# Sliding-window attention and a gated convolution feed-forward: token halves in the lead-in, two-bank score tiles, and convolution blocks that change engine

## The chip, the cores and the metric

The kernel runs on one core of one Trainium2 chip. Its engines work in parallel, each on its own queue and in the order of that queue: TensorE (PE) multiplies matrices, VectorE (DVE), ScalarE (ACT) and GpSimd (POOL) work element by element, and SyncE (SP) issues the transfers between the chip's memory and the cores' working memory. They wait for each other through semaphores. PE writes its results to PSUM, eight banks of 512 fp32 numbers for each of 128 partitions; ACT and DVE read them there. The metric is the device time of one execution in microseconds; the median of several executions counts.

## The reference, cut to what matters

```python
# q, k, v: (8, 8, 576, 64) fp32 = batch, heads, tokens, head size
scores = (q @ k.T) / sqrt(64)                  # each token sees the tokens within 32 of it
scores = where(abs(i - j) <= 32, scores, -1e9)
attn = exp(scores - max); attn = attn / sum(attn)
x = (attn @ v), heads side by side             # (8, 576, 512)

h = maximum(x @ w_in, 0)                       # w_in: 512 x 1024
conv = w[0]*h[t-1] + w[1]*h[t] + w[2]*h[t+1]   # per channel, 3 taps, zero outside
out = (h * sigmoid(conv)) @ w_out              # w_out: 1024 x 512, out fp32
```

## The kernel before, in words

**Attention of one batch.** The tokens go in tiles of 64 queries against 128 keys, because the window is 32 to each side. q and k come in through SP as fp32, are cast to bf16 by POOL (`cast_qk`, lines 286 to 287), and turned by PE with an identity (`tr_mm`) so that the head size lies on the partitions; ACT and DVE copy the turned tiles out of PSUM (`tr_copy`), ACT five of nine rows and DVE four. v is cast by POOL (`cast_v`), and a copy of it, moved by 64 tokens, is made for the odd tiles (`shift_v`, tile `vo`). A "pair" is two heads, in the two halves of the partitions. `sc_mm` computes the scores of eight of the nine tiles of a pair into two PSUM banks, one for each head, `scl_mm` those of the ninth tile of two pairs; ACT takes the exponential, one instruction for each bank (`sc_exp`, `scl_exp`); DVE multiplies with a 0/1 mask (`sc_mask`). `av_mm` (batches 2 to 7) multiplies with v, which has a column of ones beside it, so that the sum of the exponentials comes out as a 65th column; DVE takes its reciprocal (`sum_rec`) and multiplies (`av_norm`), one of each for each head. The result `xn` is turned into `xT`: for batches 2 to 7 by a transposing transfer on SP's queue (`xt_dma`), for batches 0 and 1 by PE and ACT (`xt_mm`, `xt_copy`). In these two the multiplication with v goes by blocks of 128 tokens over all heads (`avc_mm`, `avc_norm`).

**Feed-forward.** Two batches make three chunks of 384 tokens, so there are twelve chunks. For each of the eight blocks `m` of 128 channels, `ph_mm` gives x @ w_in (four matmuls), ACT writes the relu to `hT`, the convolution follows, ACT takes a tanh, and DVE makes the gated product `gT` (`gate`). Then `py_mm` multiplies with w_out, three times eight matmuls, ACT copies the result (`y_copy`) and SP stores it. Chunks 0 and 1 go in two halves of 192 tokens.

**Three ways of the convolution** (`conv_by`, lines 824 to 827). On PE, three matmuls of 384 columns with diagonal matrices (`pc_mm`; the 24 diagonals are made by ACT, `make_diag`). On DVE, ACT makes the first tap and DVE adds two more (`conv_acc`). On POOL, five instructions in working memory (`conv_pool`). Chunks 0 and 1 have all blocks on PE; in the others the lists of lines 820 to 822 decide.

**What sets the order.** No order is written out. Every step is given to a planner (`Planner`, lines 27 to 136) with its engine, an estimated duration, a due time (`want`) and what it depends on. The planner lays the steps out over the engines with these estimates: among the steps that could start first it takes the one that is due first. It also hands out the PSUM banks (`takes`, `gives`) and puts filler matmuls on PE (`fill`) where PE would be idle in the first 30 us. The instructions are then issued in that order on each engine. So a change of estimates or due times (`want_of_b`, `chunk_at`, `S2`, `POOL_LAG`) changes the order everywhere. Loads of q, k, v and the weights stand in one list (`loads`, lines 646 to 656) and go to SP's queue in its order: all of batch 0, w_in, all of batch 1, w_out, and then batch by batch. There is one staging tile for each of q and k halves and for v blocks, so a load waits for the cast of the batch before.

The instructions all carry line 214, that of the helper which issues them; they are told apart by their tiles.

Of the kernel before, what the change touches and what calls it, by code (L numbers as in the profile page):

```python
# [26 lines left out]
class Planner:  # L27
# [16 lines left out]
    def run(self, fill, until):  # L44
# [17 lines left out]

        def slots_at(op):
            at = 0.0
            for name, n in op.takes:
                pool = self.free[name]
                if len(pool) < n:
                    return None
                at = max(at, pool[n - 1][0])
            return at  # L70

        done = 0
        while done < len(ops):
# [30 lines left out]
            for name, n in op.takes:  # L104
                got = self.held[key, name] = [self.free[name].pop(0)[1] for _ in range(n)]
                self.after.setdefault(key, []).extend(self.given.get((name, x)) for x in got)
# [33 lines left out]
def kernel(  # L140
# [27 lines left out]
    ROWS = 2  # L168
# [13 lines left out]
    qT_pp = [pp.tile([128, 2, S], BF16, name=f"qT{i}") for i in range(2)]  # L182
    kT_pp = [pp.tile([128, 2, S + 2 * PAD], BF16, name=f"kT{i}") for i in range(2)]
# [5 lines left out]
    rec_pp = [pp.tile([128, 8], FP32, name=f"rec{i}") for i in range(6)]  # L189
# [12 lines left out]
    warm = pp.tile([128, 512], BF16, name="warm")  # L202
    pf = [psum.tile([128, 512], FP32, name=f"pf{i}") for i in range(8)]
# [29 lines left out]
    scalar.activation(warm[:, 256:512], warm[:, 0:256], AF.Exp, bias=0.0, scale=0.0)  # L233
# [13 lines left out]
    for t_ in kT_pp:  # L247
        vector.memset(t_[:, :, 0:PAD], 0.0)
        vector.memset(t_[:, :, PAD + S:], 0.0)
# [20 lines left out]
    QK, V96, V128, WQ = 1.55, 1.0, 1.2, 1.45  # L270
# [52 lines left out]
    def head(pr, e):  # L323
        return 4 * (pr // 2) + pr % 2 + 2 * e

    def rows_of(part):
        return range(CUT) if part == 0 else range(CUT, RP)

    def tr_mm(b, y, i, part, ps):
        nat = qkb_pp[b % 2][y][i]  # L330
        for n, j in enumerate(rows_of(part)):
            tensor.transpose(
                pf[ps[0]][:, :].bitcast(BF16)[:, 128 * n:128 * n + 128],
                nat[:, j, :, :].rearrange("p e d -> p (e d)"), ident,
            )

    def tr_copy(b, y, i, part, engine, ps):
        js = rows_of(part)
        t_ = (qT_pp, kT_pp)[y][(2 * b + i) % 2]
        to = (t_ if y == 0 else t_[:, :, PAD:PAD + S]).rearrange(  # L340
            "p y (x j) -> p y x j", j=RP)[:, :, :, js[0]:js[-1] + 1]
        from_ = pf[ps[0]][:, :].bitcast(BF16)[:, 0:128 * len(js)].rearrange(
            "p (j y x) -> p y x j", j=len(js), y=2)
# [5 lines left out]
    def score(gi, z, e, t, to):  # L349
        qT, kT = qT_pp[gi % 2], kT_pp[gi % 2]  # L350
        tensor.matmul(
            to,
            kT[64 * e:64 * e + 64, z, 64 * t:64 * t + 128],
            qT[64 * e:64 * e + 64, z, 64 * t:64 * t + 64],
# [13 lines left out]
    def sc_exp(g, e, ps):  # L368
        scalar.activation(
            attn_pp[g // 2 % 2][:, g % 2, e, 0:512], pf[ps[e]], AF.Exp, bias=0.0, scale=scale  # L370
        )

    def scl_exp(gi, e, ps):
        scalar.activation(
            attn_pp[gi % 2][:, :, e, 512:576],
            pf[ps[e]][:, 0:128].rearrange("p (z x) -> p z x", z=2), AF.Exp, bias=0.0, scale=scale,
# [7 lines left out]
    def av_mm(g, ps):  # L384
# [3 lines left out]
        for e in range(2):  # L388
            for c in range(NBLK):
                for j in range(2):  # L390
# [4 lines left out]
                        (ve if t % 2 == 0 else vo)[:, t // 2, head(pr, e), :],  # L395
# [7 lines left out]
    def av_norm(g, e, ps, r):  # L403
        b, pr = g // NP, g % NP
        po = pf[ps[e]][:, 0:65 * NBLK].rearrange("p (c x) -> p c x", x=65)
        rec = rec_pp[r][:, 0:NBLK]
        vector.tensor_tensor(
            out=xn_pp[b % 2][:, :, head(pr, e), :], in0=po[:, :, 0:64],
            in1=rec[:, :, None].broadcast_to([128, NBLK, 64]), op=ALU.mult,
        )  # L410

    def avc_mm(b, c, e, ps):
        ve, vo = ve_pp[b % 2], vo_pp[b % 2]
        for pr in range(NP):
            attn = attn_pp[pr // 2][:, pr % 2]
            for j in range(2):
                t = min(2 * c + j, NT - 1)
                tensor.matmul(
                    pf[ps[0]][64 * j:64 * j + 64, 65 * pr:65 * pr + 65],
                    attn[:, e, 64 * t:64 * t + 64],  # L420
                    (ve if t % 2 == 0 else vo)[:, t // 2, head(pr, e), :],
                    start=True, stop=True,
                )

    def avc_norm(b, c, e, ps, r):
        po = pf[ps[0]][:, 0:65 * NP].rearrange("p (a g x) -> p a g x", a=2, g=2)
        rec = rec_pp[r][:, 0:NP]
        to = xn_pp[b % 2][:, c, :, :].rearrange("p (a e g) d -> p e a g d", a=2, e=2)[:, e]
        vector.tensor_tensor(
            out=to, in0=po[:, :, :, 0:64],  # L430
            in1=rec.rearrange("p (a g) -> p a g", a=2)[:, :, :, None].broadcast_to([128, 2, 2, 64]),
# [49 lines left out]
    def relu(c, m, part, ps):  # L481
# [14 lines left out]
        scalar.activation(to, from_, AF.Relu, bias=0.0, scale=0.5)  # L496
# [83 lines left out]
    NSH = 8  # L580
    VP = 2
# [6 lines left out]
    MO, ME = 7.0, 9.0  # L588
# [3 lines left out]
    S2 = 52.0  # L592
# [10 lines left out]
    DIAG_T = 14.0  # L603
# [28 lines left out]
    for m in range(MB):  # L632
        for kk in range(3):
            engine = "ACT"
# [6 lines left out]
    loads = []  # L641

    def add_load(key, cost, fn, deps=()):
        add(key, "SP", -1.0, 0.5, fn, deps, dma=cost)

    for b in range(B):
        for i in range(NPH):
            for y in range(2):
                loads.append((("load", b, y, i), QK, lambda b=b, y=y, i=i: load_qk(b, y, i),
                              [("cast", b - 1, y, i)]))  # L650
        for c in range(NBLK):
            loads.append((("loadv", b, c), V96 if c in (0, NBLK - 1) else V128,
                          lambda b=b, c=c: load_v(b, c), [("castv", b - 1, c)]))
        if b < 2:
            for x in range(4):
                loads.append((("load w", b, x), WQ, None, [("setup sp",)]))

    return_to = {}

    def want_of_b(b):  # L660

        if b == 0:
            return 4.0, 14.0
        if b == 1:
            return 18.0, 34.0
# [5 lines left out]
    for n, (key, cost, fn, deps) in enumerate(loads):  # L671
# [5 lines left out]
        else:  # L677
            at = 0.01 * n if b < 2 else want_of_b(b)[0] - 22.0 + (n - 8) % 13 * LD
            add(key, "SP", at, 0.5, fn, deps + [("issue", prev), ("setup sp",)]
# [18 lines left out]
    for b in range(B):  # L698
# [3 lines left out]
        avs = lambda bb: ([("avc", bb, c, e) for c in range(NBLK) for e in range(2)] if bb < 2  # L702
                          else [("av", bb * NP + p) for p in range(NP)])
        for i in range(NPH):
            for y in range(2):
                add(("cast", b, y, i), "POOL", t0 + 2 * i * d - 6.0 + y, 1.16,
                    lambda b=b, y=y, i=i: cast_qk(b, y, i),
                    [("load", b, y, i)] + [("tr", b - 2, y, i, part) for part in range(2)] + ([("setup pool",), ("setup dve",)]))
        for c in range(NBLK):
            add(("castv", b, c), "POOL", t0 - 2.0 + 1.5 * c, 0.6, lambda b=b, c=c: cast_v(b, c),  # L710
                [("loadv", b, c), ("vo", b - 2, 0), ("vo", b - 2, 1)]
                + [("voc", b - 2, x, h) for x in range(NBLK - 1) for h in range(2)] + avs(b - 2))
        if b < NSH:
            for c in range(NBLK - 1):
                for h in range(2):
                    engine = ("DVE", "ACT")[(c + h) % 2] if b == 0 else "POOL" if b >= VP else "DVE"
                    add(("voc", b, c, h), engine, t0 + 0.5 * c + (2.0 if engine == "POOL" else 9.0),
# [9 lines left out]
        for i in range(NPH):  # L727
            gi = 2 * b + i
            before = avs(b - 1) if 0 < b < 3 else [("av", 2 * gi - 4), ("av", 2 * gi - 3)]
            used = [("sc", 2 * gi - 4), ("sc", 2 * gi - 3), ("scl", gi - 2)]  # L730
            for y in range(2):
                tt = t0 + 2 * i * d + 0.35 * d * y
                for part in range(2):
                    n = 128 * len(rows_of(part))
# [15 lines left out]
            for e in range(2):  # L750
                add(("expl", gi, e), "ACT", ts + 0.02 + 0.01 * e, act(128),
                    lambda gi=gi, e=e: scl_exp(gi, e, ps_of(("scl", gi))),
                    [lk] + before, gives=[("p", lk, e)])
            for z in range(2):
# [5 lines left out]
                for e in range(2):  # L760
                    add(("exp", g, e), "ACT", ts + 0.01 * e, act(512),
                        lambda g=g, e=e: sc_exp(g, e, ps_of(("sc", g))),
                        [sk] + before, gives=[("p", sk, e)])
# [3 lines left out]
                    [("exp", g, e) for e in range(2)] + [("expl", gi, e) for e in range(2)]  # L767
                    + [("setup pool",)], shared=True)
                if not cmajor:
# [7 lines left out]
                    for e in range(2):  # L777
                        rk = ("rec", g, e)
                        add(rk, "DVE", ta + 0.01, 0.11,
                            lambda r, ak=ak, e=e: sum_rec(NBLK, ps_of(ak)[e], r[0]), [ak],  # L780
                            takes=[("rec", 1)])
                        add(("norm", g, e), "DVE", ta + 0.02, dve(320),
                            lambda g=g, e=e, ak=ak, rk=rk: av_norm(g, e, ps_of(ak), held[rk, "rec"][0]),
                            [rk] + [("xt", b - 2, c) for c in range(NBLK)],
                            gives=[("p", ak, e), ("rec", rk, 0)])
        for c in range(NBLK):
            xdeps = [("ph", (b // 2 - 2) * 3 + z, m, part) for z in range(3) for m in range(MB)
                     for part in (None, 0, 1)]
            if cmajor:
                tx = t1 + 0.9 * c  # L790
                for e in range(2):
                    ak = ("avc", b, c, e)
# [175 lines left out]
```

## Time and profile before

| | us |
|---|---|
| median of 3 runs | 230.41 (229.62 to 232.28) |
| the profiled execution | 230.19 |
| its span, first to last instruction | 228.3 |

| engine | busy us | share of the span | instructions |
|---|---|---|---|
| PE | 216.6 | 95% | 2633 |
| ACT | 194.2 | 85% | 460 |
| POOL | 178.8 | 78% | 202 |
| DVE | 176.2 | 77% | 407 |

The profile is of one execution. A row names the engine, the operation, the tile that is written and those that are read, and the shape. In the rows of groups stand the count, after the bar the busy time and the mean duration of one, and after the second bar the idle time of the engine just before them with what ended it. Matmuls are pipelined and the ends that the profile shows are modelled, so a busy PE can be one that waits shortly between matmuls. "Granted clock" (PEclk) is the share of TensorE's full clock that the chip allowed.

### The profile page before, as it was taken

The numbers are of one execution on the slowest core, as the hardware profiler recorded it, in microseconds if no ns is written. First come the engines' busy times: TensorE is split into PE (matmuls) and PEld (weight loads), VectorE is DVE, ScalarE is ACT, GpSimd is POOL, SyncE is SP. The second block draws the span as 40 slices with busy tenths as digits, with TensorE's granted clock in tenths as the row PEclk, the third lists the DMA queues.
The fourth block names the chain that finished last, engine by engine and source line by source line (L and its number), as shares of the span: only waits on it lengthen the run. The fifth ranks groups of instructions, "written<-read, shape, count | busy, mean of one in ns | idle before, by whom it ended". The sixth has DMA issues, their size and how long they took to land.

```text
span 228.3 us, 6942 instructions
## 1 busy us (share of the span) xinstructions
PE 216.6 (95%) x2633; PEld 140.1 (61%) x2656; DVE 176.2 (77%) x407; ACT 194.2 (85%) x460; POOL 178.8 (78%) x202
## 2 busy tenths in 40 slices
PE   7887997999999999999999999999999999999994
PEld 6786986868665555656555565555556555555542
DVE  4389279769779897959889799859889898877620
ACT  4979799967989878999899898899899978989841
POOL 5574766878989939998989999899789679899400
PEclk9999799999999999999999999999999999999999
DMA  6999999989971579979989487569936403421213
GB/s 227 298 229 377 330 224 354 383 177 296 304 185 46 95 258 342 200 173 328 318 232 289 103 221 194 95 215 318 240 88 103 141 15 95 137 93 46 92 49 138
DMA packets 69590, 45.95 MB, mean 201 GB/s; under 512 B 53533, under 2 KB 55861, under 8 KB 69557
## 3 DMA queue, kind: packets, MB, share of 16 engines
q1 hardware_dynamic: 69520, 45.49, 70.2%
q8 instruction: 21, 0.34, 0.7%
q14 instruction: 13, 0.10, 0.1%
q10 hardware_dynamic: 36, 0.01, 0.0%
HBM read 32.52 MB, written 9.44 MB: 184 GB/s over the span
## 4 chain that ended last, share of the span: by engine, by line
PE 72%; POOL 7%; DVE 7%; ACT 4%; DMA 4%; issue 3%; SPq 1%; DVEq 0%; POOLq 0%; ACTq 0%
PE pf L214 72%; DMA kst<-in_k_dram 4%; POOL vo L214 3%; DVE gT L214 2%; POOL ca L214 1%; ACT hT L214 1%; ACT pf L214 1%; POOL ve L214 1%; DVE pf L214 1%; DVE attn L214 1%; DVE vo L214 1%; POOL cb L214 1%; ACT attn L214 1%; POOL kb L214 1%; SPq L214 1%
## 5 line engine op out<-in xcount | busy, mean ns | idle before, releaser
L214 PE MATMUL pf<-xT,w_in_sb 128*128 128x385 bf16 (+3 forms) x448 | 77.7, 309 | 1.6 <-DVE gT L214 0.8
L214 DVE SCALAR_TENSOR_TENSOR gT<-pf,hT 128x384 bf16<-128x384 f32 (+1 forms) x112 | 53.5, 495 | 19.1 <-ACT pf L214 18.3
L214 PE MATMUL pf<-w_out_sb,gT 128*128 128x512 bf16 (+1 forms) x273 | 66.1, 373 | 1.2
L214 ACT ACTIVATE hT<-pf 128x385 bf16<-128x385 f32 (+3 forms) x112 | 49.8, 465 | 5.9 <-PE pf L214 5.0
L214 PEld LDWEIGHTS <-w_in_sb 128*128 128x128 bf16 x448 | 40.5, 99 | 20.3 <-issue 1.9
L214 ACT ACTIVATE pf<-pf 128x384 f32<-128x384 f32 (+1 forms) x100 | 43.5, 448 | 4.3 <-PE pf L214 2.4
L214 PEld LDWEIGHTS <-gT 128*128 128x128 bf16 x296 | 28.4, 98 | 28.8
L214 ACT ACTIVATE attn<-pf 128x512 bf16<-128x512 f32 (+1 forms) x96 | 41.4, 509 | 0.9 <-PE pf L214 0.8
L214 DVE SCALAR_TENSOR_TENSOR pf<-hT,conv_w_sb,pf 128x384 f32<-128x384 bf16 x62 | 37.9, 617 | 4.2 <-ACT pf L214 3.7
L214 PE MATMUL pf<-hT,diag_w 128*128 128x384 bf16 (+1 forms) x207 | 36.3, 289 | 1.0 <-ACT hT L214 0.7
L214 DVE TENSOR_TENSOR attn<-attn,mask 128x1152 bf16<-128x1152 bf16 x32 | 29.0, 916 | 6.5 <-ACT attn L214 6.3
L214 POOL TENSOR_SCALAR vo<-ve 64x520 bf16<-64x520 bf16 x48 | 31.0, 646 | 3.7
L214 POOL TENSOR_SCALAR cb<-hT,conv_w_sb 128x384 f32<-128x384 bf16 x24 | 33.2, 1385 | 0.4
L214 ACT COPY y<-pf 128x512 f32<-128x512 f32 (+1 forms) x36 | 21.0, 584 | 11.2 <-PE pf L214 10.8
L214 POOL TENSOR_SCALAR ve<-vst 128x512 bf16<-128x512 f32 x40 | 27.2, 686 | 4.0 <-DMA vst<-in_v_dram 2.0
L214 DVE TENSOR_TENSOR xn<-pf,rec 128x320 bf16<-128x320 f32 (+1 forms) x68 | 28.7, 463 | 0.5 <-DVE rec L214 0.4
L214 POOL TENSOR_TENSOR ca<-ca,cb 128x384 f32<-128x384 f32 x24 | 23.8, 996 | 1.1
L214 POOL TENSOR_SCALAR qb<-qst 128x1152 bf16<-128x1152 f32 x16 | 19.7, 1233 | 5.9 <-DMA qst<-in_q_dram 5.6
L214 PEld LDWEIGHTS <-diag_w 128*128 128x128 bf16 x207 | 17.9, 98 | 9.7 <-issue 1.6
L214 POOL TENSOR_SCALAR kb<-kst 128x1152 bf16<-128x1152 f32 x16 | 18.5, 1159 | 5.1 <-DMA kst<-in_k_dram 3.6
L214 POOL TENSOR_SCALAR ca<-hT,conv_w_sb 128x384 f32<-128x384 bf16 x12 | 15.7, 1305 | 8.2 <-ACT hT L214 7.6
L214 ACT ACTIVATE pf<-hT,conv_w_sb 128x384 f32<-128x384 bf16 x31 | 18.4, 595 | 0.3
(47 smaller groups left out, 240.7 us busy)
## 6 DMA issues: line engine op xcount, KB each, us to landing
qst<-in_q_dram SPq DMA_DIRECT2D x16, 576.0 KB, 6.9
kst<-in_k_dram SPq DMA_DIRECT2D x16, 576.0 KB, 7.9
out_dram<-y SPq DMA_DIRECT2D x35, 256.0 KB, 2.2
vst<-in_v_dram SPq DMA_DIRECT2D x24, 256.0 KB, 5.3
vst<-in_v_dram SPq DMA_DIRECT2D x16, 192.0 KB, 4.9
wst<-in_moe_w_in_dram SPq DMA_DIRECT2D x4, 512.0 KB, 5.7
wst<-in_moe_w_out_dram SPq DMA_DIRECT2D x4, 512.0 KB, 7.5
xT<-xn SPq DMA_TRANSPOSE x30, 2.5
```

The lines of the kernel that those rows point to most:

```text
L214: return lambda *args, **kwargs: fixed(do(*args, **kwargs))
```

## The change

**Lead-in of batches 0 and 1 in halves of the tokens.** q and k are loaded by token halves for all eight heads (two transfers for each, `load_qk`) where they were loaded by head halves for all tokens. The order on SP is q and k of the first half, three v blocks, q and k of the second half, two v blocks, then w_in; for batch 1 two loads of w_out stand before its second half and two after. Each half is turned, scored (`sch_mm`, four tiles of two pairs in one step, or five tiles of one pair), exponentiated, masked and multiplied with v for itself: blocks 0 and 1 of 128 tokens follow the first half, blocks 2 to 4 the second. ACT copies three of nine rows of the turned tiles there and DVE six. The four shifted copies of v that ACT made for batch 0 go to DVE. qT and kT are one tile each. Due times of these steps are `HALF_AT`, `FF_AT`, `FF_STEP`.

**Two heads in adjacent banks.** The eight banks are four tiles of two. A step that takes two banks gets an aligned pair; a step that takes one prefers a bank whose neighbour is taken. One exponential, one reciprocal and one multiplication serve both heads, with twice the elements.

**Convolution blocks.** The lists go by chunk. They put 52 blocks of chunks 2 to 11 off PE (44 on DVE, 8 on POOL); before, the lists put 43 there (31 on DVE, 12 on POOL).

The estimates and due times change with it (`S2` 52 to 54, `MO`/`ME`, `POOL_LAG` 10 to 6, `DIAG_T`, the costs of loads, `LEAD`).

```diff
+        def pairs(pool):
+            at = {i: t for t, i in pool}
+            return sorted((max(t, at[i + 1]), i) for i, t in at.items()
+                          if i % 2 == 0 and i + 1 in at)
...
+        def take(name, n, start):
+            pool = self.free[name]
+            if n == 2:
+                i = pairs(pool)[0][1]
+                self.free[name] = [x for x in pool if x[1] not in (i, i + 1)]
+                return [i, i + 1]
...
-    pf = [psum.tile([128, 512], FP32, name=f"pf{i}") for i in range(8)]
+    pf2 = [psum.tile([128, 2, 512], FP32, name=f"pf{i}") for i in range(4)]
+    pf = [pf2[i // 2][:, i % 2, :] for i in range(8)]
...
     def load_qk(b, y, i):
+        if b < BH:
+            src = (q, k)[y][b, :, i * TH:(i + 1) * TH, :]
+            for e in range(2):
+                sync.dma_start(
+                    qkst[y][i][:, e, :, :].rearrange("p j d -> p (j d)"),
+                    bass.AP(src.tensor, src.offset + 4 * e * S * D, [[S * D, 4], [RP * D, 32], [1, RP * D]]),
+                )
+            return
...
+    def sch_mm(gi, hf, zs, ps):
+        ts = tiles_of(hf)
+        for z in zs:
+            for n in range(len(ts)):
+                for e in range(2):
+                    x = (n + e * (len(ts) // 2)) % len(ts)
+                    at = 64 * (x + len(ts) * (z - zs[0]))
+                    score(gi, z, e, ts[x], pf[ps[e]][:, at:at + 64])
+
+    def sch_exp(gi, hf, zs, ps):
+        ts = tiles_of(hf)
+        n = 64 * len(ts)
         scalar.activation(
+            attn_pp[gi % 2][:, zs[0]:zs[-1] + 1, :, 64 * ts[0]:64 * ts[0] + n].rearrange(
+                "p z e x -> p e z x"),
+            pf2[ps[0] // 2][:, :, 0:n * len(zs)].rearrange("p e (z x) -> p e z x", x=n),
+            AF.Exp, bias=0.0, scale=scale,
+        )
...
+    def sc_exp(g, ps):
         scalar.activation(
+            attn_pp[g // 2 % 2][:, g % 2, :, 0:512], pf2[ps[0] // 2], AF.Exp, bias=0.0, scale=scale
+        )
...
     def sum_rec(n, ps, r):
-        po = pf[ps][:, 0:65 * n].rearrange("p (c x) -> p c x", x=65)
-        vector.reciprocal(rec_pp[r][:, 0:n], po[:, :, 64])
+        po = pf2[ps[0] // 2][:, :, 0:65 * n].rearrange("p e (c x) -> p e c x", x=65)
+        vector.reciprocal(
+            rec_pp[r][:, 0:2 * n].rearrange("p (e c) -> p e c", e=2), po[:, :, :, 64]
+        )
...
+    HALF_AT = ((4.0, 16.0), (24.0, 30.0))
+    FF_AT = (13.0, 24.0, 38.0)
+    FF_STEP = (1.2, 1.6, 1.2)
...
+    loads = (qk_loads(0, 0) + v_loads(0, (0, 1, 2)) + w_loads(0, range(W1)) + qk_loads(0, 1)
+             + v_loads(0, (3, 4)) + w_loads(0, range(W1, 4)) + w_loads(1, range(W2))
+             + qk_loads(1, 0) + v_loads(1, (0, 1, 2)) + w_loads(1, range(W2, W3))
+             + qk_loads(1, 1) + v_loads(1, (3, 4)) + w_loads(1, range(W3, 4)))
...
-    BY_POOL, BY_DVE = (0,), (1, 3, 5)
-    LATE_POOL, LATE_DVE = (0, 2), (1, 3, 4, 6)
-    LAST_POOL, LAST_DVE = (0,), (1, 3)
+    POOL_LAG = 6.0
+    ON_POOL = {2: (), 3: (0,), 4: (), 5: (0,), 6: (0,), 7: (), 8: (0,), 9: (0, 2), 10: (0, 2), 11: ()}
+    ON_DVE_2 = (1, 3, 5, 6)
+    ON_DVE_3 = (1, 2, 4, 5, 6)
+    ON_DVE_4 = (1, 3, 4, 6)
+    ON_DVE_5 = (1, 3, 4, 6)
+    ON_DVE_6 = (1, 2, 4, 5, 6)
+    ON_DVE_7 = (2, 4, 6)
+    ON_DVE_8 = (1, 2, 4, 5, 6)
+    ON_DVE_9 = (1, 3, 4, 5, 6)
+    ON_DVE_10 = (1, 3, 4, 5, 6)
+    ON_DVE_11 = (1, 2, 4, 5)
```

More of the change, by code (lines that the diff above doesn't have):

```diff
@@ L167 @@
     NCH = 3 * B // 2
-    ROWS = 2
+    BH = 2
+    TH = S // 2
     NCA = 3
@@ L749 @@
                 lat=PL, takes=[("p", 2)])
[L750 to L753, printed above, removed]
+            add(("expl", gi), "ACT", ts + 0.02, act(256),
+                lambda gi=gi: scl_exp(gi, ps_of(("scl", gi))),
+                [lk] + before, gives=[("p", lk, 0), ("p", lk, 1)])
             for z in range(2):
```

327 lines of the change are left out of this document (194 added, 133 removed).

## The prediction

> **What bounds the kernel now.** The first view is the page, its engine line and two of its slice rows (40 slices of 5.7 us; digits are tenths).
>
> ```profile
> PE 216.6 (95%) x2633; PEld 140.1 (61%) x2656; DVE 176.2 (77%) x407; ACT 194.2 (85%) x460; POOL 178.8 (78%) x202
> ...
> PEclk9999799999999999999999999999999999999999
> DMA  6999999989971579979989487569936403421213
> ```
>
> TensorE (PE) looks like the only bound, but a busy PE is not one at its peak. So the second view cuts the span at three events that the timeline shows: the first feed-forward matmul, the first relu of chunk 2 (385 wide), and the first of chunk 11.
>
> ```profile
> 23.02 1.45 PE L214 MATMUL pf<-xT,w_in_sb 128*128 128x193 bf16 x8 [0.45 <-ACT xT L214]
> ...
> 65.82 0.50 ACT L214 ACTIVATE hT<-pf 128x385 bf16<-128x385 f32 x1
> ...
> 207.54 0.50 ACT L214 ACTIVATE hT<-pf 128x385 bf16<-128x385 f32 x1
> ```
>
> The busy time of each engine in these four stretches:
>
> ```profile
> core 0: us, PE busy (x) PEld busy (x) DVE busy (x) ACT busy (x) POOL busy (x), PEclk, DMA share, GB/s
> 0.00:23.00 23.00, 18.43 (x361) 16.59 (x362) 15.34 (x52) 18.55 (x43) 13.18 (x22) 0.99 0.95 284
> 23.00:65.80 42.80, 40.62 (x606) 33.39 (x609) 31.19 (x85) 37.15 (x112) 33.15 (x42) 0.96 1.01 287
> 65.80:207.50 141.70, 140.14 (x1577) 80.72 (x1597) 121.16 (x258) 126.61 (x281) 126.28 (x135) 1.00 0.65 178
> 207.50:228.30 20.80, 17.36 (x97) 9.40 (x96) 8.47 (x16) 11.88 (x26) 6.14 (x6) 0.98 0.24 89
> ```
>
> How hard does PE really work? These are its matmuls from 200 to 210 us, where all 10.0 us are busy, and there is no attention left.
>
> ```profile
> L214 PE MATMUL pf<-w_out_sb,gT 128*128 128x512 bf16 x17 | 4.2, 379 | 0.0
> L214 PE MATMUL pf<-xT,w_in_sb 128*128 128x385 bf16 x20 | 3.4, 328 | 0.0
> L214 PE MATMUL pf<-xT,w_in_sb 128*128 128x386 bf16 x14 | 2.8, 327 | 0.0
> L214 PE MATMUL pf<-hT,diag_w 128*128 128x384 bf16 x6 | 1.3, 326 | 0.0
> ```
>
> That is 17 x 512 + 20 x 385 + 14 x 386 + 6 x 384 = 24,112 columns in 10.0 us, 2.41 per ns, so a 384-column matmul costs 0.16 us when nothing is in its way. In the long stretch the large ones are these.
>
> ```profile
> L214 PE MATMUL pf<-w_out_sb,gT 128*128 128x512 bf16 x197 | 49.9, 379 | 1.0
> L214 PE MATMUL pf<-xT,w_in_sb 128*128 128x385 bf16 x194 | 38.2, 328 | 0.0
> L214 PE MATMUL pf<-hT,diag_w 128*128 128x384 bf16 x96 | 20.8, 327 | 0.0
> L214 PE MATMUL pf<-xT,w_in_sb 128*128 128x386 bf16 x96 | 18.7, 328 | 0.2 <-DVE xn L214 0.2
> ```
>
> Their 249,474 columns at that rate are 103.5 us of 141.7. Attention's small matmuls and short waits share the other 38, and the busy figure does not part them. So the 140.14 is an upper bound of PE's work, and ACT at 126.61, POOL at 126.28 and DVE at 121.16 stand close behind. Before 23 us PE mostly waits. That makes three questions: when feed-forward starts, whether the stretch to 65.8 shortens, and which engine limits the long one.
>
> **The change, part by part.**
>
> *Start of feed-forward.* It starts at 23.02, after the whole attention of batch 0. In the new order it follows the first token half's xT and the second half's scores, so two other things can hold it: w_in and the k load of the second half.
>
> ```profile
> 10.96 1.15 POOL L214 TENSOR_SCALAR kb<-kst 128x1152 bf16<-128x1152 f32 x1 [1.02 <-DMA kst<-in_k_dram]
> ...
> 18.55 0.43 DVE L214 CAST w_in_sb<-wst 128x512 bf16<-128x512 f32 x1
> ...
> 22.68 1.20 POOL L214 TENSOR_SCALAR w_in_sb<-wst 128x512 bf16<-128x512 f32 x2 [0.75 <-DMA wst<-in_moe_w_in_dram]
> ```
>
> SP issues the same bytes before w_in as now, in 13 DMAs where it was 9, so the first quarter can be cast at about 18.6 to 19.2 and the last at 22.7. The second k goes behind three v loads, 704 KB; at 284 GB/s that is 2.5 us, so its cast moves from 10.96 to about 13.5, and transposes, copies and scores end near 17. w_in is the later one. Feed-forward starts at about 19.3, a gain of 3.7, less what a late quarter of w_in takes back. Bounds: 0 (all eight blocks need w_in's last quarter anyway, cast until 23.9) and 3.7. I take 2.5.
>
> *23 to 65.8.* ACT is busy for 37.15 of 42.8 us. From its rows there, and DVE's:
>
> ```profile
> L214 ACT ACTIVATE diag_w<-ident,conv_w_sb 128x128 bf16<-128x128 bf16 x7 | 2.5, 406 | 0.0
> ...
> L214 ACT COPY qT<-pf 128x640 bf16<-128x640 bf16 x16 | 12.6, 789 | 0.0
> L214 ACT COPY vo<-ve 64x520 bf16<-64x520 bf16 x4 | 2.5, 623 | 0.5 <-POOL ve L214 0.4
> L214 DVE COPY qT<-pf 128x512 bf16<-128x512 bf16 x16 | 11.5, 722 | 5.2 <-PE pf L214 5.1
> ```
>
> All 24 diagonals are now made before the first relu: 2.5 us leave. Each of batch 1's four transpose copies on ACT has 384 elements for 640: about 0.25 us each, 1.0 in all, and DVE's part grows from 512 to 768, +0.25 each. The four vo copies leave ACT before 23 us and cost DVE as much where it idles. With merged exponentials ACT loses some 4 of 37 us. Batch 1's first half also lets chunk 1's second part start before the rest of batch 1 is done. Its second half pays: its q and k now stand on SP's queue behind three v loads and two w_out loads (1.7 MB, 6 us at 287 GB/s) and behind the POOL casts of those; chunk 2 waits for them. DMA engines are full here (1.01), so this may eat the gain. Bounds 0 and 4; I take 2, so the lead-in gives 4.5 in all.
>
> *Paired score tiles.* Two instructions become one on two banks. No row has 1024 elements; I extrapolate.
>
> ```profile
> L214 ACT ACTIVATE attn<-pf 128x512 bf16<-128x512 f32 x64 | 35.0, 619 | 0.0
> L214 ACT ACTIVATE attn<-pf 128x128 bf16<-128x128 f32 x32 | 7.9, 288 | 0.9 <-PE pf L214 0.8
> L214 DVE TENSOR_TENSOR xn<-pf,rec 128x320 bf16<-128x320 f32 x48 | 21.2, 482 | 0.5 <-DVE rec L214 0.4
> L214 DVE RECIPROCAL rec<-pf 128x5 f32<-128x5 f32 x48 | 6.9, 176 | 1.9 <-PE pf L214 1.8
> ```
>
> On ACT (619 - 288) / 384 = 0.86 ns an element and 178 ns fixed; neighbours overlap by 619 - 35.0/64 = 72. A pair costs 2 x 547 = 1094 now, merged 178 + 883 - 72 = 989: 0.105 saved. For batches 2 to 7: 24 x 0.105, and 12 x 0.137 by the same sum for the 128s, 4.1 us. The Trainium skill ("ScalarE: Activation LUTs", "What ACT_TABLE_LOAD costs") gives 186 ns plus 0.833 an element and 93 of overlap, so 93 saved a pair; by it these merges would give 3.3. On DVE I take the same fixed part, less the norms' overlap of 482 - 21.2/48 = 40 and the reciprocals' of 176 - 6.9/48 = 32: some 0.12 saved for each of 24 norms and 0.10 for each of 24 reciprocals (estimates), 5.3 us. The price: both banks are freed after the whole exponential, the first some 0.5 us later, and single takers must leave adjacent pairs. Bounds 0 to 24 x 0.5 = 12 us if PE always stood waiting for that bank; I take 0, since seven others stand beside it.
>
> *Convolution blocks.* By the lists, off PE are 43 blocks now (31 DVE, 12 POOL) and 52 then (44 and 8). Chunks 2 to 10: PE -8, DVE +11, POOL -3.
>
> ```profile
> L214 DVE SCALAR_TENSOR_TENSOR pf<-hT,conv_w_sb,pf 128x384 f32<-128x384 bf16 x62 | 37.9, 617 | 4.2 <-ACT pf L214 3.7
> L214 ACT ACTIVATE pf<-hT,conv_w_sb 128x384 f32<-128x384 bf16 x31 | 18.4, 595 | 0.3
> L214 POOL TENSOR_SCALAR cb<-hT,conv_w_sb 128x384 f32<-128x384 bf16 x24 | 33.2, 1385 | 0.4
> L214 POOL TENSOR_TENSOR ca<-ca,cb 128x384 f32<-128x384 f32 x24 | 23.8, 996 | 1.1
> L214 POOL TENSOR_SCALAR ca<-hT,conv_w_sb 128x384 f32<-128x384 bf16 x12 | 15.7, 1305 | 8.2 <-ACT hT L214 7.6
> ```
>
> PE: 8 x 3 x 0.16 = -3.8. DVE: 11 x 2 x 0.61 = +13.4, with the merges +8.1, so 129.3 of 141.7. ACT: 11 x 0.595 = +6.5, with the merges +2.4, so 129.0. POOL: 3 x (1.305 + 2 x 1.385 + 2 x 0.996) = -18.2, so 108.1. What POOL's relief is worth shows in the chain of waits, which runs on POOL almost alone between these two rows and contains chunk 2's POOL block, dropped by the change:
>
> ```profile
> 63.70 0.82 POOL kb L214
> ...
> 79.88 1.02 POOL vo L214
> ```
>
> So DVE and ACT are then the fullest. If the fullest keeps the share that ACT has now (126.6 / 141.7 = 0.893), the stretch takes 129.3 / 0.893 = 144.8, +3.1; if PE stays the bound, -3.8. A late add on DVE delays tanh, queued on ACT with relus and exponentials behind it, and PE waits for their banks. Halfway would be -0.4; with POOL's chain gone I take -1.5.
>
> *Tail.* Chunk 11 loses one PE block, 0.48, and its ends stay matmuls of w_out: -0.3.
>
> **Sum.** -4.5 - 1.5 - 0.3 = -6.3 on the span of 228.3: 222.0. The profiled execution took 230.19, 1.9 more than its span, and 0.2 under the median of 230.41. Forecast 224.
>
> **Rivals.**
>
> *DVE becomes the bound: slower.* Now DVE reaches 121.16 / 141.70 = 85.5%, and what ends most of its idle time there is ACT's tanh:
>
> ```profile
> DVE gT L214 <- ACT pf L214: 7.9, 16, 1.0
> ```
>
> Each added block puts an ACT to DVE to DVE to ACT to DVE chain into two in-order queues. If DVE's share cannot rise, 129.3 / 0.855 = 151.2, +9.5, and with the lead-in's -4.5 and the tail's -0.3 that gives 235. It beats the other gains from a share under 0.883 on. For it: the same engine pair makes both waits. Against: POOL and PE, which also feed DVE, get lighter.
>
> *Lead-in held by DMA: about the same.* If w_in's last quarter and the delayed q and k hold everything, the lead-in gives nothing and the other terms 1 to 2: 228.2 to 229.2. For it: DMA shares of 0.95 and 1.01. Against: batch 1's attention is late because of ACT and DVE, not data.
>
> *The clock halves again.* Rows of the clock:
>
> ```profile
> 18.00:24.00 6.00, 4.50 (x108) 3.69 (x106) 5.32 (x23) 5.78 (x16) 3.60 (x6) 0.89 1.05 386
> 24.00:30.00 6.00, 6.00 (x72) 5.89 (x71) 2.02 (x5) 4.78 (x16) 3.62 (x4) 0.83 1.09 277
> ```
>
> Now it loses 6 x 0.11 + 6 x 0.17 = 1.7 us of PE time, just as feed-forward starts. If a pause brings a second such loss where PE has work, the time is 225.7. The Trainium skill ("TensorE: Matmul & The Clock Gate", "HAM oscillation — how this bites in real kernels") says an idle window of about 3.4 us halves the clock; half of 3.4 is the 1.7 above, so the trace agrees. By it, data later than the filler matmuls were planned for would be what hurts.
>
> *The change gains more.* If PE stays the bound (-3.8) and the lead-in gives its upper bounds (-7.7), 218.4.
>
> **How the numbers follow.** A measurement tells about 1% from no change: 228.1 to 232.7. Chances: forecast (220 to 228) 0.52, second clock loss 0.09, more gain 0.12, DMA-held 0.14, DVE-bound 0.13. Faster 0.72 (the first three, less 0.01 that falls short); same 0.15 (the fourth and that 0.01); slower 0.13. The range 217.5 to 231 leaves out most of the DVE case and little at the bottom.
>
> **What would show it.** Right: first w_in matmul near 19 to 20 us; chunk 2's first relu near 61; from there to chunk 11's first relu about 140; DVE busy about 187 us in all, ACT about 192, POOL about 154; merged exponential near 1.06 us. Wrong: idle time on PE ended by DVE in the long stretch, DVE's share there under 88%, the merged exponential or norm at no less than two single ones, or the second half of batch 1 waiting for kst or qst.

## The result, and the profile after

The changed kernel takes **329.51 us** (median of 4 runs, 327.59 to 331.45); the kernel before took 231.34 beside it. The ratio is 1.430, with a 95% interval of 1.423 to 1.437. The forecast was 224.0 with a range to 231, so it was wrong by a hundred microseconds, and in sign. The profiled execution has a span of 328.8 us. From its page, the busy times and two of the slice rows (40 slices, now of 8.2 us each; the DMA row is the mean busy share of the 16 DMA engines in tenths):

```profile
PE 239.2 (73%) x2659; PEld 149.9 (46%) x2659; DVE 193.2 (59%) x367; ACT 202.5 (62%) x421; POOL 151.3 (46%) x182
...
PEclk9769895978999999899999999999999779999999
DMA  2445646379495935948525984685215003201003
```

TensorE was busy for 95% of the span before and is for 73% now; no other engine has taken its place (ACT 62%, DVE 59%). Nothing became the bound: everything waits. The DMA row, which stood at 6 to 9 for the first eight slices, begins with 2445.

The same three events as before cut the span: the first feed-forward matmul and the first relus of chunks 2 and 11.

```profile
37.57 0.83 PE L237 MATMUL pf<-xT,w_in_sb 128*128 128x193 bf16 x8 [0.55 <-ACT attn L237]
...
101.63 0.50 ACT L237 ACTIVATE hT<-pf 128x385 bf16<-128x385 f32 x1 [0.39 <-PE pf L237]
...
301.19 0.49 ACT L237 ACTIVATE hT<-pf 128x385 bf16<-128x385 f32 x1 [0.22 <-PE pf L237]
```

Busy times in the four stretches of the changed kernel:

```profile
core 0: us, PE busy (x) PEld busy (x) DVE busy (x) ACT busy (x) POOL busy (x), PEclk, DMA share, GB/s
0.00:37.57 37.57, 23.39 (x328) 21.67 (x329) 12.73 (x36) 15.49 (x37) 11.36 (x20) 0.82 0.49 151
37.57:101.63 64.06, 46.77 (x645) 36.78 (x645) 35.83 (x74) 38.95 (x99) 32.68 (x42) 0.89 0.64 197
101.63:301.19 199.56, 151.32 (x1596) 82.56 (x1595) 133.28 (x238) 134.41 (x259) 107.21 (x122) 0.97 0.50 129
301.19:328.80 27.61, 17.72 (x92) 8.87 (x91) 11.33 (x21) 13.70 (x29) 0.00 (x0) 1.00 0.19 67
```

The stretches were 23.0, 42.8, 141.7 and 20.8 us. All four are longer, by 14.6, 21.3, 57.9 and 6.8. In the first the DMA moves 151 GB/s where it moved 284. In the third, the DMA has little to do with it: with faster loads (the second kernel of experiment 5) that stretch still takes about 200 us. There the waits between the engines have changed. In the kernel before, the matmuls (PE, their weight loads apart) waited there three times by the profile's list, for three different instructions on other engines. This is one of the waits, and the other two are as short (total us, times, longest):

```profile
PE pf L214 <- DVE xn L214: 0.2, 1, 0.2
```

And these are some waits of the changed kernel in its third stretch:

```profile
...
ACT pf L237 <- DVE pf L237: 16.4, 17, 2.9
PE pf L237 <- ACT pf L237: 16.3, 16, 2.6
...
PE pf L237 <- DVE gT L237: 10.2, 12, 2.1
...
DVE gT L237 <- ACT kT L237: 5.8, 3, 2.4
```

The last one is the odd one. `gT` is a product of the feed-forward, `kT` the copy of a turned key tile: neither reads what the other writes. The only thing they share is PSUM.

### The profile page after: what moved, and what is told of

Its sections match the earlier page's. It is cut to its first block, busy times and chain, and to the rows that moved or that the text cites. A ratio compares the mean times of both kernels' runs of the same rounds, so it can differ in the third digit from the quotient of the medians.

```text
span 328.8 us, 6870 instructions
## 1 busy us (share of the span) xinstructions
PE 239.2 (73%) x2659; PEld 149.9 (46%) x2659; DVE 193.2 (59%) x367; ACT 202.5 (62%) x421; POOL 151.3 (46%) x182
## 4 chain that ended last, share of the span: by engine, by line
PE 34%; ACT 19%; DVE 16%; DMA 13%; SPq 7%; issue 5%; POOL 4%; ACTq 0%; DVEq 0%; POOLq 0%
PE pf L237 34%; DMA kst<-in_k_dram 9%; ACT pf L237 8%; SPq L237 7%; DVE pf L237 6%; DVE gT L237 5%; ACT hT L237 5%; DMA qst<-in_q_dram 4%; ACT y L237 2%; ACT attn L237 2%; DVE qT L237 1%; DMA out_dram<-y 1%; POOL vo L237 1%; DVE kT L237 1%; ACT qT L237 1%
## 5 line engine op out<-in xcount | busy, mean ns | idle before, releaser
L237 PE MATMUL pf<-xT,w_in_sb 128*128 128x385 bf16 (+3 forms) x448 | 80.8, 315 | 26.2 <-ACT pf L237 11.3
L237 PE MATMUL pf<-w_out_sb,gT 128*128 128x512 bf16 (+1 forms) x296 | 70.4, 384 | 10.2 <-ACT pf L237 5.4
L237 DVE SCALAR_TENSOR_TENSOR pf<-hT,conv_w_sb,pf 128x384 f32<-128x384 bf16 x88 | 53.9, 619 | 27.3 <-PE pf L237 11.2
L237 ACT ACTIVATE hT<-pf 128x385 bf16<-128x385 f32 (+3 forms) x112 | 48.2, 448 | 23.1 <-PE pf L237 15.3
L237 PE MATMUL pf<-hT,diag_w 128*128 128x192 bf16 (+1 forms) x180 | 31.6, 293 | 12.6 <-DVE gT L237 4.3
L237 ACT ACTIVATE attn<-pf 128x1024 bf16<-128x1024 f32 (+2 forms) x48 | 37.8, 812 | 1.0 <-PE pf L237 1.0
L237 POOL TENSOR_SCALAR ca<-hT,conv_w_sb 128x384 f32<-128x384 bf16 x8 | 10.6, 1330 | 58.4 <-ACT hT L237 58.4
L237 POOL TENSOR_SCALAR ve<-vst 128x512 bf16<-128x512 f32 x40 | 25.6, 642 | 21.9 <-DMA vst<-in_v_dram 14.6
L237 DVE TENSOR_TENSOR attn<-attn,mask 128x1152 bf16<-128x1152 bf16 (+2 forms) x32 | 29.3, 923 | 9.6 <-ACT attn L237 9.5
L237 POOL TENSOR_SCALAR kb<-kst 128x1152 bf16<-128x1152 f32 x16 | 19.8, 1239 | 26.2 <-DMA kst<-in_k_dram 26.1
L237 ACT ACTIVATE pf<-hT,conv_w_sb 128x384 f32<-128x384 bf16 x44 | 25.6, 584 | 9.4 <-PE pf L237 5.2
L237 ACT COPY y<-pf 128x512 f32<-128x512 f32 (+1 forms) x36 | 20.8, 580 | 16.9 <-PE pf L237 12.7
L237 PE MATMUL pf<-ident,kb 128*128 128x128 bf16 x144 | 13.7, 241 | 21.1 <-POOL kb L237 15.8
L237 DVE TENSOR_TENSOR xn<-pf,rec 128x640 bf16<-128x640 f32 (+1 forms) x34 | 26.3, 777 | 0.3
L237 PEld LDWEIGHTS <-kb 128*128 128x128 bf16 x144 | 10.5, 108 | 23.7 <-POOL kb L237 16.6
```

What stands on the lines that cost most here:

```text
L237: return lambda *args, **kwargs: fixed(do(*args, **kwargs))
```

## Two theories, and a rival for each

**Tied banks.** The semaphore waits of this program go by declared tiles. With two banks in one tile, an instruction on one bank waits for earlier work on the other, though no data passes between them. Rival: instructions that span two banks are slow, or come too late, by themselves.

**Narrow loads.** The half loads of q and k have a source pattern whose outermost dimension is 4 (the heads), and are carried by a few DMA engines only. Rivals: halves are slow because they are more and smaller transfers, or because of their place in the queue.

A third suspect was the rule of the prediction's slower rival: convolution blocks overfill DVE.

## The experiments

**1. Declare the banks in twos and change nothing else.** In the kernel before:

```diff
-    pf = [psum.tile([128, 512], FP32, name=f"pf{i}") for i in range(8)]
+    pf2 = [psum.tile([128, 2, 512], FP32, name=f"pf{i}") for i in range(4)]
+    pf = [pf2[i // 2][:, i % 2, :] for i in range(8)]
```

Every engine has the same instructions in the same order on the same banks; only the waits differ.

> The kernel before, with nothing changed but the declaration of the PSUM tiles: four tiles of two banks, each old tile a slice of one. No instruction is merged or moved. Theory (two banks in one tile wait for each other: a reader or writer of one bank holds up the other): most of the loss is here, 280 to 330 us. Rival 1 (the longer convolution lists make DVE and ACT the bound) and rival 2 (token halves bring the data of the lead-in late): 229 to 233 us, the time before.

Measured: 300.68 us (298.75 to 310.44), ratio 1.303 [1.288, 1.318]. So two lines that compute nothing cost 69 us by themselves, of 98 that the whole change costs. From the first relu of chunk 2 to that of chunk 11, 141.7 us before, the same matmuls now take 186.55:

```profile
83.09:269.64 186.55, 150.93 (x1578) 82.66 (x1571) 125.96 (x258) 132.99 (x282) 117.91 (x129) 0.99 0.49 134
```

What ended DVE's idle time ahead of the reciprocals and the multiplications of the attention, in the kernel before:

```profile
  PE pf L214: 3.0, 4
  DVE rec L214: 0.4, 1
```

and in this one, with the same view:

```profile
  PE pf L215: 10.0, 16
  ACT y L215: 1.9, 2
  ACT pf L215: 1.3, 4
  ACT hT L215: 1.0, 2
  ACT xT L215: 0.9, 2
  DMA out_dram<-y: 0.2, 1
```

Besides longer waits for PE, these steps now wait for copies of the output (`y`), for the relu (`hT`) and once, as the profile infers it, for a store. The timeline of the same kernel shows such waits one by one, all within 2.4 us:

```profile
152.61 1.25 ACT L215 ACTIVATE attn<-pf 128x512 bf16<-128x512 f32 x3 [1.79 <-DVE xn L215]
...
153.76 0.22 PE L215 MATMUL pf<-ve,attn 128*64 128x65 bf16 x1 [2.24 <-DVE pf L215]
...
155.00 0.20 DVE L215 RECIPROCAL rec<-pf 128x5 f32<-128x5 f32 x1 [0.66 <-ACT y L215]
```

ACT stands 1.79 us behind a multiplication on DVE, PE 2.24 us behind a convolution's add on DVE, and DVE 0.66 us behind a copy on ACT. Since the engines' queues run in order, each of these stops all that is queued behind it.

**2. Tiles of four.** The same two lines with four banks in each of two tiles.

> The kernel before with its eight banks declared as two tiles of four; no instruction, bank or order differs, only the waits. Theory (an instruction on one bank waits for the work on the other banks of its tile): one neighbour a bank cost 300.7 - 231.3 = 69 us, so three neighbours cost more: 335 at the least, 440 if each neighbour costs the same. Rival (a fixed price of the three-dimensional declaration, or of a few unlucky pairs): about 300, as with tiles of two.

Measured: 493.75 us (488.82 to 495.8), ratio 2.139 [2.115, 2.163]. One neighbour a bank costs 69 us, three cost 264, more than three times as much. A fixed price of the declaration is out. Not all of the 264 are waits: the granted clock has a mean of 0.75 in that run, where it is 0.99 in the kernel before.

**3. The whole change with single banks.** Eight tiles of one bank; each merged step becomes two instructions, and the rest of the change stays.

```diff
-        scalar.activation(
-            attn_pp[g // 2 % 2][:, g % 2, :, 0:512], pf2[ps[0] // 2], AF.Exp, bias=0.0, scale=scale
-        )
+        for e in range(2):
+            scalar.activation(
+                attn_pp[g // 2 % 2][:, g % 2, e, 0:512], pf[ps[e]], AF.Exp, bias=0.0, scale=scale
+            )
```

> The changed kernel with eight tiles of one bank again: each merged exponential, reciprocal and multiplication is two instructions, one for each bank; pairs are still handed out together, token halves and convolution lists stay. Theory (shared tiles): 219 to 233 us, that is the forecast of the prediction give or take the merges. Rival 1 (convolution lists) and rival 2 (token halves): 300 us or more, since both stay in.

Measured: 259.73 us (258.88 to 261.33), ratio 1.127 [1.119, 1.135]. Untying gives back 70 us, and 28 stay: the tied banks aren't all of it.

**4. Are the 28 us the convolution blocks?** Once the new lists alone in the kernel before, once the kernel of experiment 3 with the old lists.

```diff
-    POOL_LAG = 10.0
-    BY_POOL, BY_DVE = (0,), (1, 3, 5)
...
+    POOL_LAG = 6.0
+    ON_POOL = {2: (), 3: (0,), 4: (), 5: (0,), 6: (0,), 7: (), 8: (0,), 9: (0, 2), 10: (0, 2), 11: ()}
+    ON_DVE_2 = (1, 3, 5, 6)
...
```

> The kernel before with the new convolution lists and the POOL lag of the change alone. Theory (shared tiles): 224 to 238 us. Rival 1 (convolution lists): 280 to 330 us. Rival 2 (token halves): 229 to 233 us.

> The changed kernel with one-bank tiles as before and with the old convolution lists: token halves and the new due times remain. Theory (shared tiles): 222 to 233 us. Rival 1 (convolution lists): 222 to 233 us as well. Rival 2 (token halves): 300 us or more.

Measured: the lists alone 234.23 us (232.93 to 235.5), ratio 1.015 [1.008, 1.023]; the halves alone 264.56 us (263.96 to 266.15), ratio 1.148 [1.140, 1.156]. The lists cost 3 us in the kernel before and give 4.8 beside the halves. The halves hold what is left of the loss. In steps of 6 us, the start of the kernel before:

```profile
0.00:6.00 6.00, 4.49 (x37) 3.98 (x38) 2.62 (x19) 3.07 (x7) 3.28 (x9) 1.00 0.67 233
6.00:12.00 6.00, 4.60 (x100) 4.16 (x100) 2.75 (x4) 6.00 (x16) 3.34 (x3) 1.00 1.16 280
```

and that of the halves alone, with the next step, where the granted clock (third number from the end) falls too:

```profile
0.00:6.00 6.00, 4.90 (x42) 4.65 (x43) 2.49 (x17) 3.11 (x8) 2.12 (x8) 1.00 0.16 48
6.00:12.00 6.00, 2.12 (x30) 1.95 (x29) 0.00 (x0) 1.11 (x5) 1.15 (x1) 0.80 0.43 137
12.00:18.00 6.00, 3.13 (x30) 2.87 (x29) 0.98 (x2) 1.96 (x7) 1.79 (x3) 0.50 0.55 138
```

48 GB/s for 233, while SP still has loads to issue: the transfers run, but slowly.

**5. The same half loads with the rows outermost ("wide loads").** In the kernel of experiment 3, the 32 rows of a head are put ahead of the 4 heads; bytes, count and place of the transfers stay, and the copy behind the transposition reads in the new order.

```diff
-   bass.AP(src.tensor, src.offset + 4 * e * S * D, [[S * D, 4], [RP * D, 32], [1, RP * D]]),
+   bass.AP(src.tensor, src.offset + 4 * e * S * D, [[RP * D, 32], [S * D, 4], [1, RP * D]]),
```

> As the run with one-bank tiles, but the half loads of q and k list the 32 rows outermost and the 4 heads inside them (the transposed copy reads its columns in the same new order); bytes and packet sizes stay. Theory (an access pattern with 4 outermost goes over 4 of the 16 DMA engines, so these loads run at a quarter of the rate): DMA share in the first 6 us back from 0.16 to about 0.6, first relu from 39 to near 21 us, chunk 2's first relu from 95.7 to 60 to 66 us, time 224 to 234 us. Rival (the order of the halves itself: v and w_out loads ahead of the second half, waits for the eighth transfer before): little change, 252 to 260 us.

Measured: **227.53 us** (225.5 to 229.39), ratio 0.988 [0.981, 0.994]. This is the fastest kernel of the study, and the only one that beats the kernel before, by 1.2%. One swap of two dimensions is worth 32 us here. Two more kernels have the swap: the changed kernel with nothing else mended, and the halves alone with the old lists.

> The changed kernel, two-bank tiles and merged instructions as they are, with the half loads in the new order of rows alone. If the two causes add up: 329.5 less the 30 us of the lead-in, 295 to 305 us. If the tiles make the lead-in late by themselves, so that the loads hide behind them: 315 to 330 us.

> One-bank tiles, half loads with the rows outermost, the old convolution lists: token halves alone, mended. By the prediction's sum its lead-in gains 4.5 us: 224 to 228 us. If halves gain nothing: 229 to 233 us. Against the run with the new lists it shows what these are worth here: -1.5 us by the prediction, +3 us as in the kernel before.

Measured: 303.31 us (299.95 to 305.58), ratio 1.316 [1.305, 1.326], so the swap gives 26 us in the changed kernel; and 233.05 us (232.82 to 234.07), ratio 1.016 [1.011, 1.020], 31.5 less than the halves without it.

**6. Narrow loads in the kernel before.** The first attempt wrote the 128 rows of the old loads as 4 times 32.

```diff
+        dims = [[32 * RP * D, 4], [RP * D, 32]] if b < 2 else [[RP * D, 128]]
```

> The kernel before with the same q and k loads of batches 0 and 1, byte for byte and in the same order, whose source pattern is written with an outermost dimension of 4 (4 times 32 rows) where it was 128. Theory (the outermost dimension sets how many DMA engines carry a load): the 4.7 MB of these loads go at some 137 GB/s, 34 us, where they went at some 280, 17 us; first q cast near 10 us instead of 4.8, first relu 8 to 15 us later than 23.9, in all 240 to 260. Rival (the loads of the change were slow because they are halves, or because of their place in the order): 229 to 233, first relu near 24.

Measured: 229.95 us (228.61 to 232.95), ratio 1.000 [0.995, 1.005]. This says nothing about either side: 4 steps of 32 rows are one run of 128 equal steps, and the loads ran as before. Between 4 and 8 us the trace has 16.3 packets under way at a time in both kernels. That the two dimensions were merged when the program was built is likely, but no run shows it. So the next two kernels take the rows in an order that can't be merged, in two transfers for each load. The rows of q and k of batches 0 and 1 then stand in other places, and the attention of these batches is that of other tokens, with the same work.

```diff
+        if b < 2:
+            for e in range(2):
+                sync.dma_start(
+                    qkst[y][i][:, e, :, :].rearrange("p j d -> p (j d)"),
+                    bass.AP(src.tensor, src.offset + 2 * e * S * D, [[RP * D, 4], [4 * RP * D, 32], [1, RP * D]]),
+                )
+            return
```

> The kernel before; each q and k load of batches 0 and 1 goes as two transfers of 288 KB, and in each the source rows come in steps, 4 outermost and 32 within, so the rows of a head stand in another order (what is computed with them is the same work on rows in the wrong places). No other instruction differs from the next kernel, which has 16 outermost. Theory (the outermost dimension sets how many DMA engines carry a load): the eight transfers of batch 0 go at the 70 to 140 GB/s of the half loads, first q cast near 8 to 10 us instead of 4.8, the last of batch 0 at 17 to 28 instead of 10.96, 240 to 262 us in all. Rival (halves of a load, or their place in the order, are what was slow): as the next kernel.

> As the kernel with 4 outermost, but with 16 outermost and 8 within: the same bytes, the same number of transfers, rows in another order too. Theory: all 16 DMA engines carry each load, so 229 to 233 us and a first q cast near 4 us. Rival (split transfers or stepped rows are slow by themselves): 240 or more, like the one with 4.

Measured: 263.02 us (261.92 to 264.17), ratio 1.142 [1.131, 1.152], with 4 outermost, and 234.86 us (233.29 to 236.41), ratio 1.019 [1.009, 1.030], with 16. POOL's casts of batch 0 wait for the data as follows, with 4 outermost:

```profile
10.04 1.15 POOL L214 TENSOR_SCALAR qb<-qst 128x1152 bf16<-128x1152 f32 x1 [6.67 <-DMA qst<-in_q_dram]
15.76 1.15 POOL L214 TENSOR_SCALAR kb<-kst 128x1152 bf16<-128x1152 f32 x1 [4.57 <-DMA kst<-in_k_dram]
21.85 1.15 POOL L214 TENSOR_SCALAR qb<-qst 128x1152 bf16<-128x1152 f32 x1 [4.94 <-DMA qst<-in_q_dram]
27.88 1.15 POOL L214 TENSOR_SCALAR kb<-kst 128x1152 bf16<-128x1152 f32 x1 [4.88 <-DMA kst<-in_k_dram]
```

and with 16:

```profile
5.75 1.15 POOL L214 TENSOR_SCALAR qb<-qst 128x1152 bf16<-128x1152 f32 x1 [2.39 <-DMA qst<-in_q_dram]
...
12.85 1.15 POOL L214 TENSOR_SCALAR kb<-kst 128x1152 bf16<-128x1152 f32 x1 [1.19 <-DMA kst<-in_k_dram]
```

Between 4 and 8 us the trace has 4.2 packets under way at a time with 4 outermost and 16.5 with 16, and with 4 the last cast comes 15 us later. The two kernels differ in nothing else, so neither halves nor their place are at fault. Splitting and stepping the rows costs 3.8 us against the kernel before. The Trainium skill ("DMA: Bandwidth & Descriptors", "Why a DMA increments its semaphore by 16 and not by 1") says that a transfer issued from SP runs on the largest number of DMA engines, up to 16, that divides the slowest dimension of both patterns. The trace agrees with it as far as packets under way show it: 4.2 and 16.5.

**7. Merged instructions without tied banks.** In the changed kernel with wide loads, four banks in two tiles and four single banks; a single step that takes a place in a tile takes all of it, so no two steps ever share one.

```diff
-    pf2 = [psum.tile([128, 2, 512], FP32, name=f"pf{i}") for i in range(4)]
-    pf = [pf2[i // 2][:, i % 2, :] for i in range(8)]
+    pf2 = [psum.tile([128, 2, 512], FP32, name=f"pf{i}") for i in range(2)]
+    pf = [pf2[i // 2][:, i % 2, :] for i in range(4)] + [
+        psum.tile([128, 512], FP32, name=f"pf{i}") for i in range(4, 8)]
```

> The changed kernel with half loads as above and with merged instructions, but only four banks in two-bank tiles; the other four are tiles of one bank. A step that takes one bank gets one of these, or a whole two-bank tile, whose other bank then stays empty. So no two steps ever share a tile. Theory (the loss comes from two steps in one tile): 220 to 236 us, less what fewer places cost. Rival (instructions over two banks are slow or block by themselves): 270 us or more.

Measured: 234.01 us (233.87 to 235.71), ratio 1.021 [1.016, 1.025]. The merged instructions aren't slow: the 75.8 us between this change's two kernels with wide loads (303.31 and 227.53) fall to 6.5. But no gain from them shows either. That the 6.5 us come from the fewer places that the planner has to give is likely and was not tried apart.

**The sum.** From the kernel before (229.86 beside these kernels): halves with wide loads 233.05, +3.2; new lists 227.53, -5.5; two-bank tiles and merges 303.31, +75.8; narrow loads 329.51, +26.2.

## Why the prediction was wrong, point by point

**The step that failed: the price of the paired tiles.** The prediction gave the two-bank tiles "Bounds 0 to 24 x 0.5 = 12 us" and took 0, "since seven others stand beside it". It priced when a bank comes free to the next taker. It didn't see that the tile is what waits are made from, so that the seven others don't stand beside it: each is tied to its neighbour for everything, also for steps that were never merged. The measured price is 69 us in the kernel before, 70 between experiment 3 and the whole change, 76 with wide loads. The diff showed the cause (`pf2`, four tiles); the profile before couldn't, since no two steps shared a tile.

**The second step: half loads by bytes.** The lead-in reckoned "the same bytes" in 13 transfers, and 704 KB at 284 GB/s. The rate was that of loads with 128 rows outermost; the pattern in the diff has 4. The second k cast was forecast near 13.5 us. In the changed kernel POOL casts it at 30.75:

```profile
30.75 1.15 POOL L237 TENSOR_SCALAR kb<-kst 128x1152 bf16<-128x1152 f32 x1 [4.60 <-DMA kst<-in_k_dram]
```

With the wide loads of experiment 5 it is cast at 15.36:

```profile
15.36 1.27 POOL L236 TENSOR_SCALAR kb<-kst 128x1152 bf16<-128x1152 f32 x1 [0.28 <-DMA kst<-in_k_dram]
```

The price, 26 to 32 us, lies ahead of chunk 2. In the changed kernel the first w_in matmul starts at 37.57, not at the forecast 19 to 20, and chunk 2's first relu at 101.63; with wide loads these are 23.62 and 75.04. A sign that the prediction named came too: POOL waits 6.45 us for q of batch 1's second half and 4.31 for its k. The rival "Lead-in held by DMA" had the right place, but its price was the loss of the gain, not of 26 us more.

**What the rest of the sum was worth** shows where both are mended (experiment 5), though without the merges; experiment 7 has them, with fewer places in PSUM. The stretches of experiment 5:

```profile
0.00:20.50 20.50, 18.32 (x327) 17.43 (x328) 12.75 (x40) 15.18 (x39) 10.18 (x17) 1.00 0.96 248
20.50:63.61 43.11, 41.12 (x647) 33.12 (x647) 32.93 (x90) 37.54 (x115) 32.50 (x41) 1.00 1.01 298
63.61:205.13 141.52, 139.28 (x1593) 78.76 (x1591) 130.05 (x287) 129.55 (x289) 110.98 (x124) 1.00 0.73 185
205.13:225.70 20.57, 17.15 (x96) 9.17 (x94) 10.66 (x21) 12.90 (x29) 1.55 (x2) 1.00 0.25 90
```

- *Start of feed-forward:* the forecast gain was 3.7, less what a late quarter of w_in takes back: 2.5. The start comes 23.02 - 20.50 = 2.5 earlier, but only then does the late quarter take some back: PE waits for its casts at 21.95 and 23.10, 1.26 us in all. What is left is nearer 1.3, and that the two numbers agree is luck.

```profile
21.95 0.34 PE L236 MATMUL pf<-xT,w_in_sb 128*128 128x193 bf16 x2 [0.46 <-POOL w_in_sb L236]
23.10 0.67 PE L236 MATMUL pf<-xT,w_in_sb 128*128 128x193 bf16 x6 [0.80 <-POOL w_in_sb L236]
```

- *To chunk 2:* forecast -2; measured 43.11 for 42.8, so +0.3. The lead-in gives 2.2 for 4.5. How much of this the merges would have added isn't known.
- *The long stretch:* forecast -1.5; measured 141.52 for 141.70, -0.2. That is less than this stretch differs by itself: the last two kernels of experiment 6 differ from the kernel before only ahead of it, and have 142.1 and 143.3. With the merges (experiment 7) it is 145.6. And the parts don't add: from the kernel before, the lists alone shorten nothing there (148.2 us between the same relus), the halves alone neither (147.1), and only both together come out level. Why each alone lengthens it stays open. PE's term there was -3.8, and its busy time, which the prediction rightly calls an upper bound of its work, fell by 0.9; POOL's term was -18.2 and is -15.3. DVE's and ACT's, before the merges, were +13.4 and +6.5 and are +8.9 and +2.9. The tail's was -0.3 and is -0.2.
- *DVE becomes the bound:* not in this kernel. DVE is busy for 130.05 of 141.52 us, 91.9%, where it had been 85.5%; the rival needed a share that stays under 0.883. With the lists alone it did stay under it (experiment 4: 129.75 us busy in the 147.90 from 64.10 on, 87.7%), so there the rival is not excluded; it is worth 3 us in that kernel, not 98. In the changed kernel the share is 133.28 / 199.56 = 67%, which the prediction listed as a sign of this rival. It is a sign of any stall, and this one's cause was another.
- *Busy times:* forecast 187 for DVE, 192 for ACT, 154 for POOL, with the merges. Experiment 7, which has them, comes near:

```profile
PE 219.0 (94%) x2668; PEld 139.3 (60%) x2668; DVE 187.4 (81%) x367; ACT 195.4 (84%) x421; POOL 154.8 (67%) x182
```

But experiment 5, without them, has 186.4, 195.2 and 155.2. The merges should have taken 5.3 us off DVE and 4.1 off ACT, and between these two kernels nothing goes; so DVE's agreement is in part luck.

**Merged instructions: shorter than two, by a little less than forecast.** Rows of the changed kernel:

```profile
L237 ACT ACTIVATE attn<-pf 128x1024 bf16<-128x1024 f32 x28 | 28.3, 1025 | 0.8 <-PE pf L237 0.8
L237 DVE TENSOR_TENSOR xn<-pf,rec 128x640 bf16<-128x640 f32 x24 | 19.6, 815 | 0.1
...
L237 DVE RECIPROCAL rec<-pf 128x10 f32<-128x10 f32 x24 | 5.1, 213 | 1.5 <-PE pf L237 1.5
```

The exponential takes 1.025 us (forecast near 1.06). A pair of single ones took 2 x 35.0 / 64 = 1.094 of ACT's time and a merged one takes 28.3 / 28 = 1.011, so 0.083 is saved for the forecast 0.105. For the multiplications 2 x 21.2 / 48 - 19.6 / 24 = 0.067 is saved for 0.12, for the reciprocals 2 x 6.9 / 48 - 5.1 / 24 = 0.075 for 0.10. The sign that the prediction set for its failure here, a merged instruction no shorter than two, didn't come. By these rows a merge saves less than a tenth of a microsecond; the engines' totals above show no saving at all, and it was bought with waits on every engine.

**The clock rival** came in, as a consequence: the granted clock of the first stretch is 0.82, and 0.50 from 12 to 18 us in experiment 4, where PE waits for data. The Trainium skill ("TensorE: Matmul & The Clock Gate", "HAM oscillation — how this bites in real kernels"), which the prediction cites, says that an idle window of about 3.4 us halves the clock. The trace agrees where PE starves: with the halves alone PE is idle for 3.9 us from 7.4 us on, and the clock falls to 0.50 in that time. It doesn't show that so long a pause is needed: in the kernel before, the clock stood at 0.50 from 22.66 to 26.07 us, which is the 1.7 us that the prediction reckoned, and PE's longest pause in the ten microseconds ahead of it was 1.05 us. Either way the loss here follows from the loads and goes with them (1.00 in all stretches of experiment 5).

**Range and chances.** The range could not hold the result, because no rival held either mechanism. The 0.13 for slower stood on DVE alone.

## What to carry to other kernels

Before several buffers are declared as one tile, ask what the program's waits are made from: here sharing a tile between unrelated steps cost 69 us with the instructions unchanged, and merging two instructions saves less than 0.1 by its rows. Read a changed load for its outermost dimension, not only for its bytes; a 4 there moved 48 GB/s in the first 6 us where 128 moved 233. When all engines' shares fall together, look in the waits for two names that exchange no data.

## What was not expected of the hardware

With 4 outermost, 4.2 packets were under way at a time. Each had 2,304 bytes and took 93 ns, so 4.2 x 2304 / 93 = 104 GB/s, and 102 is what the stretch from 6 to 12 us moved, with SP still issuing loads. The trace doesn't name the DMA engine of a packet; that the other twelve stood idle is read from the 4.2 alone.

In the same kernel the clock was granted at 0.50 from 12 to 24 us throughout, though PE was busy for 3.24 and 3.83 us of each 6.

```profile
6.00:12.00 6.00, 0.75 (x8) 0.76 (x9) 0.00 (x0) 0.49 (x2) 1.15 (x1) 0.68 0.26 102
12.00:18.00 6.00, 3.24 (x31) 2.98 (x30) 0.73 (x1) 1.90 (x5) 1.15 (x1) 0.50 0.37 124
18.00:24.00 6.00, 3.83 (x63) 3.48 (x62) 0.73 (x1) 3.72 (x10) 1.15 (x1) 0.50 0.31 113
```
